# Linear attention and a PReLU layer in one kernel: the order of pieces in the usual steps

## The chip, the cores and the metric

The kernel runs on one core of a Trainium2 chip. The metric is device time in microseconds (us): the median of four runs before the change is 626.19 us (626.02 to 626.37). All views of the profile come from one further execution, recorded by the hardware profiler, which took 626.12 us. TensorE does the matmuls, VectorE (DVE) and ScalarE (ACT) do elementwise work, GpSimd (POOL) and SyncE (SP) mostly issue transfers (DMAs).

## The reference

Two blocks follow each other. The first is a linear attention with a forget gate: for 4 batches and 8 heads, over 768 tokens, with 48 x 48 states,

```
f = 1 / (1 + exp(-f_logit))
for t in range(S):
    state = f[:, :, t, :, None] * state + einsum('bhd,bhe->bhde', k[:, :, t], v[:, :, t])
    y[:, :, t] = einsum('bhd,bhde->bhe', q[:, :, t], state)
```

Its output, laid out as 3072 tokens of 384 numbers, is x of the second block:

```
h = x @ w_in                                     # 384 -> 2048
g = maximum(h, 0) + alpha * minimum(h, 0)
out = g @ w_out                                  # 2048 -> 384
```

All of it is in float32.

## The kernel before, in words

**Tiles and steps.** A step takes one chunk of 128 tokens for two batches and all heads, which makes 256 rows of x. There are 6 chunks and 2 pairs of batches, so 12 steps, numbered 0 to 11 here, the pairs alternating. In pass n of the main loop (called step n below) the attention of step n runs, the second block (the network) of step n-1, and the preparation of step n+1. A pass 12 has only the last network.

**Pieces.** Each part is a Python generator, and each `yield` ends a piece. The letters stand in the strings of orders.

- Q, preparation of the next step (`prepare`), 6 pieces. Piece 1 loads f, q, k and v by GpSimd's queue, applies the sigmoid, and makes the first products (ACT L267, L268, L270; DVE L278 to L282). Piece 2 has four ScalarE copies (L302) and two scans (L305, L307). Piece 3 has L309, L335 and the first L318; piece 4 has L362, L318 and L356; piece 5 has L386, the transpose L389, the last L318, L394, L356 and the four L402. Piece 6 has four ScalarE copies into the attention matrix A (L407) and sixteen DMAs on SP that write `ksn` from `kt` (L415). P is the same generator one step later, so a piece that Q left over is run as P.
- O, `carry`, 2 pieces: the `off` matmuls (L432) with four ScalarE copies into A (L450); then the `pd` matmuls (L472), which read `ksn` and give the state's update, whose first half DVE takes (L482, L486).
- S, `attend`, 6 pieces. Pieces 1 and 2, one for each batch of the pair: `raw` matmuls (L508), DVE's masked copies of them into `ad` (L514), `qu` matmuls (L523), and masked copies (L529). Pieces 3 and 4: four ScalarE copies each from `ad` to A (L551). Piece 5: the output matmuls `py` (L562). Piece 6, the output stage: the second half of the state's update (`moved(1)`, again L482 and L486), the ScalarE copies to y (L571), and the DMAs from y to xT on SP, ACT and POOL (L591).
- n, `network`, 13 pieces. Eight are hidden tiles: `ph` matmuls from xT (L606), ScalarE's negative part (L611, into one of two `neg` buffers), and two gate operations on DVE (L613), with four sums (L687) after the fourth and the eighth tile. Five make the output by seven products of 8 matmuls (L645), named pa, pb; pc, pd; pa, pc again; pe; with DVE and ScalarE combining them (L653, L658, L662, L663, L667 to L669, L672) and two stores by SP (L621).

**What sets the order.** On TensorE, DVE and ScalarE the order is exactly that in which the pieces issue their instructions: the schedule is manual for these three. SP and POOL are ordered by the framework. Steps 0 to 3 have orders of their own (`first`), steps 4 to 12 share `usual`. A piece that isn't there any more (the preparation in step 11, the attention in step 12) is passed over.

**Buffers that tie the pieces.** PSUM has two tiles of two banks (`pair`), used in turn by raw, qu, off, pd and py: `qu` at the head of a step takes the one that `pd` of the step before held, which is read last by L486. Four single banks serve ph and the products: the first `ph` of a step takes the bank of pc, last read by L667. `ksn` and y share one SBUF buffer, and f, q, k are loaded into single buffers.

Of the kernel before, what the change touches and what calls it, by code (L numbers as in the profile page):

```python
# [31 lines left out]
def kernel(  # L32
# [106 lines left out]
    for m in range(1, NB):  # L139
        lo = UO[m] + (4 if m == 1 else 0)  # L140
        n = NB - m
# [4 lines left out]
    for half in range(2):  # L146
        for m in range(1, NQ):
            n = NQ - m
# [540 lines left out]
    def halves_of_w_out():  # L689
# [23 lines left out]
        "P5 a w P a2 O w S w a w a2 S Q S O S w Q2 S Q2 S w",  # L713
        "a2 w b w O w n2 b2 v S P v2 n2 S b v Q n b n O S2 v n b v n Q2 b v Q b n S v2 W Q W S n2 W n W",
        "n S P n2 S n W n O Q n3 O S Q n S Q n Q S2 Q n3",
        "S n3 P S Q S n O n O n4 Q S Q S Q n S Q n3",
    )
    usual = "S n2 O P n S Q n2 Q n3 O n S2 n Q S Q2 S n3"
    pieces = {key: part for keys, parts in (("aw", load_weights(w_in_sb, w_in, "w_in")),
                                            ("bv", load_weights(w_out_sb, w_out, "w_out")))  # L720
              for key, part in zip(keys, parts)}
# [77 lines left out]
```

## Time and profile before

| What | Value |
|---|---|
| median of four runs | 626.19 us |
| the profiled execution | 626.12 us |
| its span on the core | 624.2 us |
| TensorE matmul busy | 589.3 us, 94% |
| VectorE busy | 502.4 us, 80% |
| ScalarE busy | 265.5 us, 43% |
| mean granted TensorE clock | 0.997 |
| HBM over the span | 66 GB/s |

The span runs from the first to the last instruction; the rest of the execution's time lies around it. A timeline row reads: start, time taken, engine, line, operation, output and inputs, shapes, how many; in brackets the idle time before it and what ended it. In rows of stages the columns are: the stretch, its length, busy time of TensorE matmuls, weight loads, VectorE, ScalarE and GpSimd, each with its count of instructions, then clock, share of DMA, and GB/s. One fp32 matmul of the program is two matmul records.

### The profile page before, as it was taken

To read this page: it belongs to the slowest core of one execution; us is meant where nothing else is said; L and a number is where in the kernel's file an instruction comes from. 1 tells how busy PE (TensorE), PEld (TensorE's weight loads), DVE (VectorE), ACT (ScalarE), POOL (GpSimd) and SP (SyncE) were. 2 spreads that over 40 slices of the span, in tenths; PEclk is the share of its full clock that TensorE was granted. 3 is DMA by queue.
4 is the path that set the end of the run, shared out by engine and by line. 5 is a ranking of instruction groups with operands and counts; after the bars stand their busy time and mean duration, and the time that the engine had idled before them with its cause. 6 is when DMAs were issued, how large, how long until landed. Compare 5 with 4: busy or idle time off the path is not lost.

```text
span 624.2 us, 19119 instructions
## 1 busy us (share of the span) xinstructions
PE 589.3 (94%) x8220; PEld 525.3 (84%) x8220; DVE 502.4 (80%) x1013; ACT 265.5 (43%) x482; POOL 60.5 (10%) x119
## 2 busy tenths in 40 slices
PE   3458999999999999999999999999999999999997
PEld 3346876789889899889889889889889889889997
DVE  7599889999799599699699699699799799673261
ACT  6797992371441541542442443353353353222110
POOL 8020001001001001001001001001001000000000
PEclk9998999999999999999999999999999999999999
DMA  8766614313314313413313323223222310300100
GB/s 308 269 226 193 194 43 96 76 35 88 85 36 94 78 35 86 85 36 85 64 59 85 56 68 85 54 68 83 54 73 73 64 38 13 65 4 13 41 0 26
DMA packets 68116, 50.43 MB, mean 81 GB/s; under 512 B 47168, under 2 KB 60608, under 8 KB 68032
## 3 DMA queue, kind: packets, MB, share of 16 engines
q1 hardware_dynamic: 56656, 25.01, 15.3%
q0 software_dynamic: 6864, 22.35, 12.3%
q10 hardware_dynamic: 4512, 1.85, 1.4%
q8 instruction: 65, 1.06, 0.7%
q14 instruction: 19, 0.16, 0.1%
HBM read 36.21 MB, written 4.72 MB: 66 GB/s over the span
## 4 chain that ended last, share of the span: by engine, by line
PE 68%; DVE 22%; ACT 7%; issue 1%; DMA 1%; ACTq 0%; DVEq 0%
PE ph L606 37%; PE pa L645 7%; PE pc L645 7%; PE pb L645 4%; DVE us L318 3%; PE qu L523 3%; PE pe L645 2%; PE pd L645 2%; PE raw L508 2%; DVE q L356 2%; DVE us L309 1%; DVE k L335 1%; DVE vs L486 1%; DVE kt L389 1%; PE pd L472 1%
## 5 line engine op out<-in xcount | busy, mean ns | idle before, releaser
L606 PE MATMUL ph<-xT,w_in_sb 128*128 128x256 f32 x1152 | 260.2, 385 | 0.0
L606 PEld LDWEIGHTS ph<-xT,w_in_sb 128*128 128x128 f32 x1152 | 217.6, 191 | 32.5 <-issue 2.5
L611 ACT ACTIVATE neg<-ph 128x512 f32<-128x512 f32 x96 | 57.2, 597 | 199.2 <-PE ph L606 152.1
L613 DVE SCALAR_TENSOR_TENSOR gate<-neg,om,ph 128x256 f32<-128x256 f32 x192 | 81.9, 475 | 58.6 <-ACT neg L611 58.6
L645 PE MATMUL pa<-w_out_sb,gate 128*128 128x192 f32 x352 | 63.5, 333 | 0.0
L645 PE MATMUL pc<-t,S 128*128 128x192 f32 x352 | 60.9, 327 | 0.0
L645 PEld LDWEIGHTS pa<-w_out_sb,gate 128*128 128x128 f32 x352 | 56.7, 190 | 2.2 <-DVE gate L613 0.7
L645 PEld LDWEIGHTS pc<-t,S 128*128 128x128 f32 x352 | 57.8, 191 | 0.1
L514 DVE COPY_PREDICATED ad<-mraw,raw 128x256 f32<-128x256 int32 (+1 forms) x96 | 42.4, 442 | 8.3 <-PE raw L508 5.8
L529 DVE COPY_PREDICATED ad<-mquad,qu 128x224 f32<-128x224 int32 (+6 forms) x140 | 41.9, 299 | 6.2
L551 ACT COPY A<-ad 32x256 f32<-32x256 f32 x96 | 38.6, 402 | 1.4
L571 ACT COPY y<-py 128x512 f32<-128x512 f32 x24 | 12.9, 588 | 58.0 <-PE py L562 57.9
L318 DVE TENSOR_TENSOR us<-us,fs 128x768 f32<-128x768 f32 (+5 forms) x60 | 36.8, 613 | 0.3
L302 ACT COPY us<-qd 128x256 f32<-128x256 f32 x48 | 29.8, 671 | 7.7 <-DVE qd L275 7.4
L687 DVE TENSOR_TENSOR S<-gate 128x512 f32<-128x512 f32 x44 | 30.3, 688 | 0.8
L645 PE MATMUL pb<-t,gate 128*128 128x192 f32 x176 | 30.4, 327 | 0.0
L645 PE MATMUL pd<-w_out_sb,S 128*128 128x192 f32 x176 | 30.4, 327 | 0.0
L645 PE MATMUL pe<-w_out_sb,S 128*128 128x192 f32 x176 | 30.4, 327 | 0.0
L508 PEld LDWEIGHTS raw<-qd,k 48*32 48x32 f32 x1536 | 18.3, 109 | 14.1 <-issue 8.5
L562 PEld LDWEIGHTS py<-A,vs 128*64 128x64 f32 x768 | 25.1, 145 | 5.8 <-issue 2.2
L407 ACT COPY A<-q 48x512 f32<-48x512 f32 x44 | 27.1, 617 | 6.4 <-DVE q L356 5.8
L508 PE MATMUL raw<-qd,k 48*32 48x80 f32 x1536 | 23.3, 244 | 6.9 <-ACT A L450 5.2
(109 smaller groups left out, 741.8 us busy)
## 6 DMA issues: line engine op xcount, KB each, us to landing
w_out_raw<-in_w_out SPq DMA_DIRECT2D x8, 767.8 KB, 4.6
w_in_raw<-in_w_in SPq DMA_DIRECT2D x8, 767.2 KB, 9.8
q<-in_qT POOLq DMA_DIRECT2D x11, 512.0 KB, 4.0
f<-in_fT POOLq DMA_DIRECT2D x11, 512.0 KB, 4.1
k<-in_kT POOLq DMA_DIRECT2D x11, 512.0 KB, 4.3
out<-o SPq DMA_DIRECT2D x24, 192.0 KB, 2.1
vs<-in_v POOLq DMA_DIRECT2D x22, 192.0 KB, 3.5
ksn<-kt SPq DMA_DIRECT2D x80, 32.0 KB, 2.0
```

What stands on the lines that cost most here:

```text
L302: nc.scalar.copy(q4[:, :, :, r], qdv[r][:, :, :, 0])
L318: nc.vector.tensor_tensor(us[:, :, UO[m]:UO[m] + 4 * n].rearrange("p g (i r) -> p g i r", r=4), us[:, :, skip:skip + 4 * n].rearrange("p g ...
L407: nc.scalar.copy(A[halves(cc)[1], :, par * HP:(par + 1) * HP, CH * cc:CH * (cc + 1)], q3[rows(par)].rearrange("p (u h c) s t -> p u h c (s ...
L508: nc.tensor.matmul(raw[DB * j:DB * (j + 1), par, hp * C:hp * C + QW], lhsT=k[r_, g * DB:(g + 1) * DB], rhs=qd[r_, g], start=True, stop=True)
L514: nc.vector.copy_predicated(adu[:, :, :, d:4], mraw[:, d, :, d:4].bitcast(I32).unsqueeze(1).broadcast_to((128, H, NB, n)), rv[:, :, QO[d]: ...
L529: nc.vector.copy_predicated(ad[:, u, :, :, 4 * m:DB], mquad[:, lo:lo + n].bitcast(I32).unsqueeze(1).unsqueeze(1).broadcast_to((128, 2, HP, ...
L551: nc.scalar.copy(A[s_, u, :, s_], ad[s_, u].rearrange("p r h t -> p (r h) t"))
L606: nc.tensor.matmul(ph[:, j * T:(j + 1) * T], lhsT=w_in_sb[:, kt, m * 128:(m + 1) * 128], rhs=xT[:, kt], start=(kt == 0 and j == 0), stop=( ...
L611: nc.scalar.activation(neg, phv, AF.Relu, scale=-1.0)
L613: nc.vector.scalar_tensor_tensor(gate[:, m % NH, m // NH], neg[:, j], om[:, m:m + 1], phv[:, j], ALU.mult, ALU.add)
L645: nc.tensor.matmul(to[:, 0:DH], lhsT=of(f), rhs=by(f), start=(f == 0 and not more), stop=(f == NH - 1), skip_group_check=True)
L687: nc.vector.tensor_tensor(to, x_, y_, op)
```

## The change

The strings of orders change; nothing else does. In the usual steps:

- The second attend piece comes before the `off` piece, and both carry pieces come between single hidden tiles, with no P.
- Preparation piece 1 comes after five hidden tiles (before: after three), piece 2 after all eight (before: after five), piece 3 right after the first output piece of the network and ahead of both copy pieces of attend.
- The copies to A and `py` (S3) come together ahead of pc and pd; before, `py` came after them.
- The output stage comes after preparation piece 4; before, it came after piece 5. Piece 5 and piece 6 follow within the same step, between the last pieces of the network.

Step 3 runs piece 6 ahead of its last two network pieces, so that step 4 finds it done.

```diff
         "n S P n2 S n W n O Q n3 O S Q n S Q n Q S2 Q n3",
-        "S n3 P S Q S n O n O n4 Q S Q S Q n S Q n3",
+        "S n3 P S Q S n O n O n4 Q S Q S Q n S Q n Q n2",
     )
-    usual = "S n2 O P n S Q n2 Q n3 O n S2 n Q S Q2 S n3"
+    usual = "S n2 S n O n O n Q n3 Q n Q S3 n Q S n Q n Q n"
```

## The prediction

> **What bounds the kernel now.** I read the engine shares and the chain on the page first, then cut the span into the kernel's steps (each from its first `raw` matmul to the next step's), then TensorE's rows at the seams, then the queues that feed them.
>
> ```profile
> PE 589.3 (94%) x8220; PEld 525.3 (84%) x8220; DVE 502.4 (80%) x1013; ACT 265.5 (43%) x482; POOL 60.5 (10%) x119
> ...
> PE 68%; DVE 22%; ACT 7%; issue 1%; DMA 1%; ACTq 0%; DVEq 0%
> ```
>
> TensorE bounds it; VectorE's 22% of the chain says that TensorE is held somewhere. By step (start:end, length, TensorE busy, its weight loads, VectorE):
>
> ```profile
> 155.27:202.65 47.38, 47.09 (x657) 42.73 (x657) 43.07 (x93) 17.89 (x35) 4.46 (x7) 1.00 0.31 71
> 202.65:249.56 46.91, 46.91 (x657) 42.62 (x656) 38.97 (x79) 18.48 (x35) 4.45 (x7) 1.00 0.26 66
> 249.56:297.28 47.72, 47.32 (x657) 42.64 (x657) 41.18 (x86) 18.54 (x35) 4.45 (x7) 1.00 0.29 68
> 297.28:344.97 47.69, 47.28 (x657) 42.64 (x656) 41.16 (x86) 18.54 (x35) 4.45 (x7) 1.00 0.27 68
> ...
> 487.71:535.05 47.34, 47.29 (x657) 42.64 (x656) 40.85 (x86) 18.57 (x35) 1.80 (x3) 1.00 0.18 39
> 535.05:581.87 46.82, 46.82 (x657) 42.82 (x657) 23.60 (x56) 13.43 (x28) 1.07 (x2) 1.00 0.14 30
> ```
>
> Step 3 is the first row; the usual order is used by steps 4 to 11, the others. Steps 4 to 10 take 332.40 us, 47.49 each. TensorE at a usual seam, then at the seam after step 3:
>
> ```profile
> 344.97 0.92 PE L508 MATMUL raw<-qd,k 48*32 48x80 f32 x64
> 346.29 1.08 PE L523 MATMUL qu<-us,k 48*32 48x112 f32 x64 [0.40 <-DVE vs L486]
> ```
> ```profile
> 186.93 1.27 PE L562 MATMUL py<-A,vs 128*64 128x64 f32 x36
> 188.49 1.04 PE L562 MATMUL py<-A,vs 128*64 128x64 f32 x28 [0.29 <-ACT A L551]
> ...
> 202.65 0.85 PE L508 MATMUL raw<-qd,k 48*32 48x80 f32 x60
> 203.28 0.26 PE L523 MATMUL qu<-us,k 48*32 48x112 f32 x1
> ```
>
> `qu` begins 1.32 after `raw` where 0.69 is its own pace (308.46 to 309.15): 0.63 lost, at five seams (steps 5 to 9); step 10 loses 0.28. The releaser is the state update of L486, which empties the `pd` bank that `qu` takes; in these steps it stands on VectorE behind preparation pieces 4 and 5. Step 3 runs it between them, and its seam has no wait; but its `py` waits on ScalarE's copies into A, since the copies of L302 stand ahead of them:
>
> ```profile
> 184.44 0.32 ACT L653 COPY Csum<-pa 128x192 f32<-128x192 f32 x1 [1.95 <-PE pa L645]
> 184.77 2.19 ACT L302 COPY us<-qd 128x256 f32<-128x256 f32 x4
> 186.76 1.68 ACT L551 COPY A<-ad 32x256 f32<-32x256 f32 x4
> ```
>
> **The change, part by part.** No instruction is added or removed; t counts from a step's first `raw`.
>
> *TensorE without waits.* Starts of one group to the next, from steps 3 and 6: raw 0.69, qu 1.00, ph0-1 5.38, raw 0.69, qu 1.00, ph2 2.79, off 0.68, ph3 2.79, pd 0.86, ph4-7 10.46 (three take 7.87, one more 2.59), pa 2.60, pb 2.69, py 2.01, pc 2.70, pd, pa and pc 2.60 each, pe 2.69: sum 46.83. The step is worth more only by what makes TensorE wait.
>
> *The seam (output stage sooner).* Old cost 0.63 x 5 + 0.28 = 3.43 us, plus up to 0.23 in `pa`, which waits in some steps for the last gates. New: L658 starts 0.27 after pc, then piece 4 (L362 to L318: 0.60+0.74+0.60+0.60+0.60+0.59 = 3.73), then L482/L486 (2.13); so L486 is done at t 43.1, and `qu` (t 47.9) doesn't wait for it. What is late next is `ph0`: its bank is emptied by L667, which now stands behind L662 and piece 5 (0.34+0.72+1.17+0.17+0.60+0.71+0.74 = 4.45). L667 ends at t 48.2, `ph0` of the next step starts at 48.9: 0.7 of slack. `qu` itself needs piece 5's last L318, done at 45.9.
>
> *Second attend half sooner.* raw at t 7.07 needs the four L514 of the first half, done at 3.8; off (11.55) needs the second four, done at 10.5; pd (15.0) needs the seven L529, done at 12.8. VectorE then idles until gate 3, so delays from before end here. Price nothing; a VectorE later by over 1.0 would show at off.
>
> *Piece 1 and the copies of L302, nearer to `py`.* This is where the new wait arises. ph3 starts at 12.23, and its ScalarE pass (L611) 2.95 later (547.34 to 550.29 in step 11): 15.18. From there VectorE is continuous: gate +0.63, its pair 0.91 to the sums, sums 2.64, L482/L486 2.19, gate pair 0.80, piece 1 3.60 (315.36 to 318.96), gate 5 ends 0.87 later. The L611 of ph7 needs that `neg` buffer, 0.11 later: 15.18 + 11.75 = 26.93. ScalarE then: L302 0.49 later (27.42), four L302 and L653 up to the first L551 2.26 (136.74 to 139.00), eight L551 3.34 (327.48 on): 33.02, TensorE awake 0.06 later at 33.08. `py` starts at 26.34 + 2.60 + 2.69 = 31.63 and comes to the matmul that needs the last L551 1.10 later, 32.73 (step 3 stopped at the same one). Wait 0.35, and 0.05 of restart as in step 3 (`py` 2.52 there, 2.01 elsewhere, for 0.46 of wait): 0.40. Bounds: nothing at all, and step 3's 0.51. I take 0.40, as its links are rows of the very instructions. Step: 46.83 + 0.40 = 47.23.
>
> *Piece 6 inside the step ahead.* ScalarE's four L407 (0.63 each) leave the place before ph2's L611, run at t 46.9 to 49.4 and finish before the next L611 (51.7): hidden under pe and the seam. SP: its program order becomes four of the sixteen `ksn` DMAs, store o1, twelve `ksn`, store o0 (before: seven, both stores, nine). So store o1's wait for L669 (t 48.8) now holds twelve `ksn` issues. Sixteen took 11.2 (4.84 + 6.38), 0.70 each: the last issues at 57.1, which is 9.9 of the next step, and lands 2.0 later (4.5 is the longest seen); pd wants it at 15.0. Hidden, by 3.1 or 0.6. The wait of the `ksn` writes for the xT DMAs (they read y, in the same buffer) is over by t 42.
>
> *DMAs that follow the moved pieces.* POOL's k load is issued after the second raw, at t 8.0 instead of 12.4 (309.68 in step 6); its readers come at 33. q goes out after L270 (t 22.1), f after L309 (33.4), vs and the xT moves after `py`: all 10 us or more ahead of their readers. xT leaves 3 us sooner than before, and ph0 did not wait for it then. Price nothing.
>
> ```profile
> k<-in_kT POOLq DMA_DIRECT2D x11, 512.0 KB, 4.3
> ...
> ksn<-kt SPq DMA_DIRECT2D x80, 32.0 KB, 2.0
> ```
>
> *Sum.* Step 4, which had no wait at its head: 47.23 - 46.91 = +0.32. Steps 5 to 9: 236.15 against 238.15, -2.00. Step 10: 47.23 against 47.34, -0.11. Step 11 has nothing to prepare, so no L302 and no wait, and its pe takes 2.60: 46.74 against 46.82, -0.08. Step 3 keeps its wait and its seam, step 12 is untouched. Total -1.87. The profiled execution took 626.12 (span 624.20 and 1.92 around it): 624.25. The median of the runs, 626.19, is 0.07 higher, within the spread of the runs: **624.3**.
>
> *Against a rule.* The seam's gap repeats, 0.40 to 0.41 idle at each. The Trainium skill (Perfetto Trace Analysis, Optimization Strategy) says that the same gap repeating on the engine that should be saturated can mean too little PSUM for the next tile. Taken so, an order that keeps two `pair` tiles keeps the gap, and the sum would be 0.40 x 7 - 0.1, or 2.7 more than now, some 628.8, against 624.3 by the rows. Step 3 has the same two tiles and no gap, so I follow the row.
>
> **The rivals.**
>
> *The copies come in time.* If the ScalarE run is 0.4 shorter, TensorE never waits: 46.83 a step, 7 x 46.83 + 46.74 = 374.6 against 332.40 + 46.82 = 379.2: 621.5. For it: the wait is the difference of two sums of some 33 us. Against: step 3 waited.
>
> *The wait is as in step 3 or longer.* 0.51 gives 47.34 a step, a gain of 1.1, 625.0; with 0.66 the step is the old mean, and all is given back: 626.1. For it: eight copies stand behind L302, where step 3 had four. Against: there L302 began only after L653, here before it.
>
> *Nothing is removed.* If VectorE reaches L486 too late after all, the seam stays: 626 to 629. Against: 4.8 us of slack.
>
> *Slower: `ksn` lands late.* The k load now runs at t 8.0 to 13, across the last `ksn` DMAs, which no usual step of before shows. If the last `ksn` is held for the whole 4.3 of the k load, it lands at 9.9 + 2.0 + 4.3 = 16.2, pd waits 1.2, and the `py` wait shrinks to the 0.05: step 48.08, +4.1 in all, 630.2. It decides from a pd wait of about 0.8, a landing 6 us after its issue; the longest seen is 4.5. The Trainium skill (DMA: Bandwidth & Descriptors, Issuing engines are not separate DMA queues) says that DMAs of all issuers interleave on the same sixteen engines; with that page's fit (Anatomy of one DMA) of 2.0 us plus bytes over 436 GB/s the k load would, as an estimate, hold the others for 1.2, not 4.3, and pd would not wait: 624.3 again. No row of this trace shows the two together.
>
> **How the numbers follow.** Forecast (a `py` wait of 0.25 to 0.5) 0.52; copies in time 0.13; a longer wait 0.17; nothing removed 0.05; `ksn` late or another late wait 0.13. A measurement of this kernel tells about 0.2%, 1.25 us, from no change, so faster ends at 624.9, a wait of 0.49. Faster: 0.46 of the forecast and 0.13, 0.59; same: 0.06 + 0.17 + 0.05, 0.28; slower 0.13. Range 621.5 (no wait) to 626.2 (all given back), leaving out the late `ksn`; the forecast's own is 623.2 to 625.0.
>
> **What would show it.** Right: `qu` starts 0.69 to 0.7 after `raw` in steps 5 to 10, without L486 as releaser; a wait of 0.2 to 0.3 idle in `py` on A (L551) in steps 4 to 10, none in step 11; steps of 47.1 to 47.35 us; the four L302 just ahead of L653. Wrong: `py` waiting 0.5 or more, a wait of `ph` on L667 or of `pd` on `ksn`, or steps of 46.9.

## The result, and the profile after

| | median | lowest to highest | runs |
|---|---|---|---|
| kernel before | 626.30 us | 624.27 to 628.31 | 71 |
| changed kernel | 625.13 us | 623.38 to 626.76 | 46 |

The ratio is 0.9981, with a 95% interval of 0.9976 to 0.9987: 0.8 to 1.5 us are gone, at about the 0.2% that this kernel can be told by. The forecast was 624.3, in a range of 621.5 to 626.2. The profiled execution has a span of 623.2 us, 1.0 below that of before.

The page of the changed kernel, shares of the engines and of the chain that ended last:

```profile
PE 588.0 (94%) x8220; PEld 525.7 (84%) x8220; DVE 503.1 (81%) x1013; ACT 260.5 (42%) x482; POOL 62.7 (10%) x119
PE 61%; DVE 19%; ACT 14%; issue 4%; DMA 1%; ACTq 0%; DVEq 0%
```

VectorE's share of the chain fell from 22 to 19%, ScalarE's rose from 7 to 14%: one wait has gone and another has come. The stages of the changed kernel, steps 3, 4, 6, 7, 10 and 11 (start:end, length, TensorE busy, weight loads, VectorE, ScalarE, GpSimd, clock, DMA share, GB/s):

```profile
155.30:202.68 47.38, 47.10 (x657) 42.73 (x656) 42.95 (x92) 20.26 (x39) 4.46 (x7) 1.00 0.31 71
202.68:249.90 47.22, 47.07 (x657) 42.71 (x657) 40.04 (x79) 15.55 (x33) 4.46 (x7) 1.00 0.28 66
...
297.24:344.61 47.37, 47.25 (x657) 42.88 (x656) 41.25 (x86) 17.80 (x36) 4.45 (x7) 1.00 0.29 68
344.61:392.01 47.40, 47.26 (x657) 42.87 (x657) 41.29 (x86) 17.79 (x36) 4.46 (x7) 1.00 0.31 69
...
486.52:533.85 47.33, 47.20 (x657) 42.83 (x656) 39.93 (x85) 19.97 (x39) 1.80 (x3) 1.00 0.19 40
533.85:580.84 46.99, 46.99 (x657) 42.87 (x657) 23.64 (x55) 11.11 (x25) 1.07 (x2) 1.00 0.13 29
```

Step 3 is as it was. Steps 4 to 11 take 378.16 us (580.84 less 202.68) against 379.22 before: 1.06 less, where 1.87 was forecast. A usual step is 47.22 to 47.40 where before had one of 46.91, five near 47.6 and one of 47.3.

TensorE's timeline of the changed kernel at the seam into step 6:

```profile
297.24 0.85 PE L508 MATMUL raw<-qd,k 48*32 48x80 f32 x60
...
297.96 1.16 PE L523 MATMUL qu<-us,k 48*32 48x112 f32 x62
299.05 0.48 PE L606 MATMUL ph<-xT,w_in_sb 128*128 128x256 f32 x1
```

`qu` begins inside the run of `raw`, 0.64 to 0.72 after it, and no bracket names L486: the seam wait is gone. VectorE ahead of this seam:

```profile
291.98 1.12 DVE L486 TENSOR_TENSOR vs<-vs,pd 48x384 f32<-48x384 f32 x2
...
297.83 0.36 DVE L667 TENSOR_TENSOR Csum<-pc,Csum 128x192 f32<-128x192 f32 x1
```

L486 ends at 293.10, 4.8 ahead of `qu`. The price is to be seen on ScalarE, and then on TensorE, in the same step:

```profile
324.33 0.60 ACT L611 ACTIVATE neg<-ph 128x512 f32<-128x512 f32 x1 [2.35 <-DVE gate L613]
324.82 2.18 ACT L302 COPY us<-qd 128x256 f32<-128x256 f32 x4
326.79 0.37 ACT L653 COPY Csum<-pa 128x192 f32<-128x192 f32 x1
327.07 3.33 ACT L551 COPY A<-ad 32x256 f32<-32x256 f32 x8
```
```profile
329.06 2.43 PE L562 MATMUL py<-A,vs 128*64 128x64 f32 x64
331.42 0.76 PE L645 MATMUL pc<-t,S 128*128 128x192 f32 x3
```

L302, L653 and the eight copies run without a gap, the last copy ends at 330.40, and `py` lasts 2.36 (329.06 to 331.42) instead of 2.01. The releaser that the waits of the weight loads name (in all, times, longest; from step 4 on) is the copy; a wait of up to 0.3 in seven of eight steps:

```profile
PEld py L562 <- ACT A L551: 1.8, 7, 0.3
```

### The profile page after: what moved, and what is told of

Its sections match the earlier page's. It is cut to its first block, busy times and chain, and to the rows that moved or that the text cites. A ratio compares the mean times of both kernels' runs of the same rounds, so it can differ in the third digit from the quotient of the medians.

```text
span 623.2 us, 19118 instructions
## 1 busy us (share of the span) xinstructions
PE 588.0 (94%) x8220; PEld 525.7 (84%) x8220; DVE 503.1 (81%) x1013; ACT 260.5 (42%) x482; POOL 62.7 (10%) x119
## 3 DMA queue, kind: packets, MB, share of 16 engines
q0 software_dynamic: 6864, 22.35, 12.5%
q8 instruction: 65, 1.06, 0.7%
## 4 chain that ended last, share of the span: by engine, by line
PE 61%; DVE 19%; ACT 14%; issue 4%; DMA 1%; ACTq 0%; DVEq 0%
PE ph L606 25%; PE pc L645 9%; PE pa L645 6%; PE pe L645 5%; PE pd L645 5%; ACT A L551 4%; ACT us L302 3%; DVE gate L613 3%; PE qu L523 3%; DVE S L687 3%; PE raw L508 3%; DVE qd L275 3%; PE py L562 2%; ACT neg L611 2%; DVE vs L482 1%
## 5 line engine op out<-in xcount | busy, mean ns | idle before, releaser
L645 PE MATMUL pa<-w_out_sb,gate 128*128 128x192 f32 x352 | 61.0, 327 | 0.0
L645 PEld LDWEIGHTS pa<-w_out_sb,gate 128*128 128x128 f32 x352 | 58.0, 190 | 0.6
L663 ACT COPY o<-pa 128x192 f32<-128x192 f32 x11 | 3.5, 318 | 75.3 <-PE pa L645 72.3
L562 PE MATMUL py<-A,vs 128*64 128x64 f32 x768 | 28.8, 233 | 3.4 <-ACT vs L488 1.3
L508 PEld LDWEIGHTS raw<-qd,k 48*32 48x32 f32 x1536 | 18.4, 109 | 13.9 <-issue 8.3
```

What stands on the lines that cost most here:

```text
L508: nc.tensor.matmul(raw[DB * j:DB * (j + 1), par, hp * C:hp * C + QW], lhsT=k[r_, g * DB:(g + 1) * DB], rhs=qd[r_, g], start=True, stop=True)
L562: nc.tensor.matmul(py[64 * par:64 * par + 64, u, o:o + CH], lhsT=vs[bp][:, cc, u, hd * D:hd * D + 64], rhs=A[:, u, par * HP + hp, CH * cc: ...
L645: nc.tensor.matmul(to[:, 0:DH], lhsT=of(f), rhs=by(f), start=(f == 0 and not more), stop=(f == NH - 1), skip_group_check=True)
```

## The experiments

All are orders of the same pieces. "The changed line" is

```
usual = "S n2 S n O n O n Q n3 Q n Q S3 n Q S n Q n Q n"
```

and `first[3]` is step 3's line. The sums below are read from the traces like those above; "head" is the time from a step's first `raw` to its first `ph` (1.69 without a wait).

| Kernel | steps 4 to 11, us | ratio to before (95%) |
|---|---|---|
| before | 379.22 | |
| changed | 378.16 | 0.9981 (0.9976 to 0.9987) |
| changed, once more | 378.22 | 0.9993 (0.9981 to 1.0004) |
| output stage alone | 377.22 | 0.9958 (0.9943 to 0.9973) |
| piece 6 in the next step | 378.63 | 0.9980 (0.9970 to 0.9990) |
| copies behind L653, L302 | 390.59 | 1.0173 (1.0144 to 1.0202) |
| L653 behind the copies | 376.46 | 0.9951 (0.9936 to 0.9967) |
| copies first | 376.13 | 0.9933 (0.9920 to 0.9947) |
| copies first, step 3 too | 375.56 | 0.9937 (0.9921 to 0.9953) |
| the same, once more | 375.87 | 0.9939 (0.9926 to 0.9952) |
| the same, k load later | 376.30 | 0.9944 (0.9927 to 0.9960) |
| the same, `off` beside `pd` | 380.75 | 1.0015 (1.0004 to 1.0026) |

**The output stage alone** (against the kernel before). Theory: the seam gap is the order on VectorE. Rival: too few `pair` tiles.

```diff
-    usual = "S n2 O P n S Q n2 Q n3 O n S2 n Q S Q2 S n3"
+    usual = "S n2 O P n S Q n2 Q n3 O n S2 n Q S Q S Q n3"
```

> The order of before with one move: the last gated output piece of a usual step (L658, L662, L667) stands ahead of preparation piece 4 instead of behind piece 5; pieces 1, 3 and 6 stay where before had them, and so does L302 on ScalarE. My theory (the seam gap was only the order on VectorE): L486 ends some 4 us ahead of qu, so qu begins 0.69 to 0.71 after raw in steps 5 to 10 without L486 as its releaser, and 0.63 a step comes back there. What is late next is L667, since VectorE has a longer run behind it: a wait of ph0 on L667 of 0 to 0.4. Steps 5 to 9 at 47.0 to 47.4 instead of 47.6, no py wait on A; 624.0 to 625.3 in all, ratio 0.9965 to 0.999. Rival (too few pair tiles in PSUM, whatever the order): the gap of 0.4 before qu stays or moves to ph0 in full, and the time stays at 626.3 within 0.5.

Measured: 624.31 us, ratio 0.9958. No wait on L486 is left, with the same two tiles; the rival falls. What is late next is L667, as the theory had it. VectorE of this kernel at the seam into step 6, and its weight loads' waits from step 4 on:

```profile
297.91 0.72 DVE L402 TENSOR_TENSOR f<-ps 48x8 f32<-48x8 f32 x4
298.64 0.36 DVE L662 TENSOR_TENSOR o<-Csum,pd 128x192 f32<-128x192 f32 x1
298.91 0.35 DVE L667 TENSOR_TENSOR Csum<-pc,Csum 128x192 f32<-128x192 f32 x1
```
```profile
PEld ph L606 <- DVE Csum L667: 2.2, 6, 0.4
...
PEld pa L645 <- DVE gate L613: 0.9, 4, 0.2
```

L667 ends at 299.26 and `ph` starts at 299.32, which makes the head 1.94, 0.25 over its own pace, in five steps. (The edit moves the output stage behind preparation piece 4; the lines that the expectation names for it, L658, L662 and L667, belong to the network.) The surprise is that this one move beats the whole change. Its waits are smaller: 1.36 at the heads and 1.15 in `pa`, 2.51 in all; in the changed kernel 0.52 at the heads, 0.32 in the second `raw` and `qu`, 2.64 in `py`, 3.48. Without them the steps of both take 46.84: (377.22 - 2.51) / 8 and (378.16 - 3.48) / 8. The wait in `pa` is counted from 2.70, since this is what it takes right behind the small matmuls of `pd` when no gate is late (behind `ph` it takes 2.60). Step 11 of this kernel, from 559.70 to 562.40:

```profile
558.84 0.94 PE L472 MATMUL pd<-vs,ksn 64*48 64x48 f32 x64
559.70 2.87 PE L645 MATMUL pa<-w_out_sb,gate 128*128 128x192 f32 x16
562.40 2.76 PE L645 MATMUL pb<-t,gate 128*128 128x192 f32 x16
```

In the other usual steps it takes 2.78 to 2.93.

**Piece 6 back in the next step.**

```diff
-        "S n3 P S Q S n O n O n4 Q S Q S Q n S Q n Q n2",
+        "S n3 P S Q S n O n O n4 Q S Q S Q n S Q n3",
-    usual = "S n2 S n O n O n Q n3 Q n Q S3 n Q S n Q n Q n"
+    usual = "S n2 P S n O n O n Q n3 Q n Q S3 n Q S n Q n2"
```

> The changed kernel with preparation piece 6 (four L407 on ScalarE, its ksn DMAs on SP) back at the head of the next step, as before had it; the output stage and pieces 1 to 5 stay as the change put them. My theory (completing the preparation inside the step ahead neither costs nor gains, all of it is covered): within 0.4 us of the changed kernel, 624.7 to 625.5, ratio to before 0.9975 to 0.9988; qu at 0.69 to 0.71, py at 2.3 to 2.4 as there. It also shows whether qu0's 1.07 to 1.10 instead of 1.00 in steps 5 to 10 comes from piece 6's work beside it: at 1.00 the steps would be 0.1 shorter and the time 0.6 lower. Rival (the ksn DMAs between the stores cost something): 1 us or more below the changed kernel; rival (completing the preparation early is where the gain comes from): back at 626.3.

Measured: 625.55 us, ratio 0.9980, that of the changed kernel. Completing the preparation inside the step ahead neither gains nor costs in the time. The heads are 1.71 to 1.81, so the small excess of `qu` there doesn't come from piece 6. One step has a `pd` of 1.48 instead of 0.87 with `ksn` as its releaser; its `py` takes 2.07, nearly without a wait, as the prediction's rival said it would.

**The copies later.** Theory: `py` waits for the end of the ScalarE run, so what is put ahead adds one for one.

```diff
-    usual = "S n2 S n O n O n Q n3 Q n Q S3 n Q S n Q n Q n"
+    usual = "S n2 S n O n O n Q n3 n Q2 S3 n Q S n Q n Q n"
```

> The changed kernel with the pass of ph7 (L611), which waits for its neg buffer, issued ahead of L302 and the eight A copies in such an order that L302 stands behind L653, as in step 3. My theory (py waits for the end of the ScalarE run L302, L653, L551, so what is put ahead of it adds one for one): the first L551 begins some 2 us later than in the changed kernel, the last ends at 35, py waits some 2.2 instead of 0.3 in steps 4 to 10: 12 to 14 us more than the changed kernel, 637 to 639, ratio to before 1.017 to 1.021. Rival (py's loss is not that run): 625 within 0.5. Between the two, if L302 starts as soon as in the changed kernel because its operands come no later: a wait of 0.3 to 1, 625 to 630.

Measured: 637.36 us, ratio 1.0173. ScalarE, then TensorE, of step 6 of this kernel:

```profile
330.04 0.32 ACT L653 COPY Csum<-pa 128x192 f32<-128x192 f32 x1 [1.64 <-PE pa L645]
330.25 2.20 ACT L302 COPY us<-qd 128x256 f32<-128x256 f32 x4
332.24 3.36 ACT L551 COPY A<-ad 32x256 f32<-32x256 f32 x8
```
```profile
333.13 0.34 PE L562 MATMUL py<-A,vs 128*64 128x64 f32 x4 [0.53 <-ACT A L551]
333.97 1.18 PE L562 MATMUL py<-A,vs 128*64 128x64 f32 x32 [0.50 <-ACT A L551]
335.65 1.03 PE L562 MATMUL py<-A,vs 128*64 128x64 f32 x28 [0.50 <-ACT A L551]
```

The last copy ends at 335.60, 34.9 after the step's start at 300.66 (35 was expected). `py` starts 0.59 late (3.29 after `pb` instead of 2.69) and takes 3.49 instead of 2.01: 2.07 a step. Steps 4 to 11 are 12.43 longer than in the changed kernel, of 12 to 14 expected.

**L653 behind the copies.** The copies stand behind two things, L302 and L653. Which of them?

```diff
-    usual = "S n2 S n O n O n Q n3 Q n Q S3 n Q S n Q n Q n"
+    usual = "S n2 S n O n O n Q n3 Q S2 n Q S n Q S n Q n Q n"
```

> The changed kernel with the eight copies into A (L551) issued between the copies of L302 and L653: L302 stays ahead of them, L653 (which waits for pa and takes 0.3) goes behind. It asks which of the two makes py late. Theory A, from the rows of the changed kernel (L302 ends at t 29.6 and L653, let go by pa at 29.2, would end at 29.6 without it, so each alone holds the copies to about 29.6 and both to 29.8): py takes 2.15 to 2.25 in steps 4 to 10 instead of 2.32 to 2.38, as step 11, which has L653 but no L302, takes 2.21; 0.8 to 1.2 us below the changed kernel, ratio to before 0.9960 to 0.9972. Theory B (L302 alone, as I predicted): py stays at 2.3 to 2.4 and the time at that of the changed kernel. Theory C (L653 alone): py 2.01 and 2.3 us or more.

Measured: 623.94 us, ratio 0.9951. ScalarE and `py` in step 6 of this kernel:

```profile
325.40 2.19 ACT L302 COPY us<-qd 128x256 f32<-128x256 f32 x4
327.35 3.36 ACT L551 COPY A<-ad 32x256 f32<-32x256 f32 x8
330.74 0.32 ACT L653 COPY Csum<-pa 128x192 f32<-128x192 f32 x1
```
```profile
329.61 2.19 PE L562 MATMUL py<-A,vs 128*64 128x64 f32 x64
331.73 1.57 PE L645 MATMUL pc<-t,S 128*128 128x192 f32 x8
```

`py` takes 2.12 to 2.15 in six of the seven usual steps (here 329.61 to 331.73), so L302 alone makes 0.11 to 0.14 of the 0.31 to 0.37. In step 7 it takes 2.01, behind a `pd` of 1.17. And in step 11, which has no L302, `py` falls from 2.21 to 2.02 with L653 out of the way: L653 alone makes 0.2. Theory A is the nearest, neither B nor C, though `py` lies a little under its 2.15 to 2.25; steps 4 to 11 are 1.70 shorter than in the changed kernel, more than its 0.8 to 1.2.

**The copies first.** Both out of the way: the last four copies ahead of the pass of ph6.

```diff
-    usual = "S n2 S n O n O n Q n3 Q n Q S3 n Q S n Q n Q n"
+    usual = "S n2 S n O n O n Q n S2 n2 Q n Q S n Q S n Q n Q n"
```

> The changed kernel with one move: the last four copies into A (L551) are issued ahead of the pass of ph6 (L611) and of L302 and L653 instead of behind them. My theory (py waits because L302 and L653 run ahead of the last A copies on ScalarE): the last L551 ends 2 us or more before py comes to it, py takes 2.01 again in steps 4 to 10 instead of 2.32 to 2.38, no releaser L551 is left in the usual steps, and 0.3 to 0.35 a step come back: 2.1 to 2.5 us less than the changed kernel, 622.6 to 623.0, ratio to before 0.994 to 0.9955. Rival (the longer py is not that queue but slower matmuls, or another operand): py stays above 2.25 and the time at 625.1 within 0.4; second rival: the copies' price moves to another wait (L653 later holds pa, L611 of ph6 later holds a neg buffer), and the gain is under 0.8.

Measured: 622.94 us, ratio 0.9933. ScalarE in step 7 of this kernel:

```profile
366.36 0.59 ACT L611 ACTIVATE neg<-ph 128x512 f32<-128x512 f32 x1
366.85 3.32 ACT L551 COPY A<-ad 32x256 f32<-32x256 f32 x8
...
371.85 2.19 ACT L302 COPY us<-qd 128x256 f32<-128x256 f32 x4
373.83 0.37 ACT L653 COPY Csum<-pa 128x192 f32<-128x192 f32 x1
```

The copies end at 370.17, 5.8 ahead of `py` (375.96), which takes 2.01 or 2.02 in all usual steps. Nothing else became late but the head of step 11, by 0.1, and `pd` in step 5, and the latter is the wait that the prediction named as the slower rival. TensorE of this kernel there:

```profile
264.66 0.30 PE L472 MATMUL pd<-vs,ksn 64*48 64x48 f32 x6
265.35 0.89 PE L472 MATMUL pd<-vs,ksn 64*48 64x48 f32 x58 [0.39 <-DMA ksn<-kt]
```

It costs 0.63 (1.50 for 0.87); with no `py` wait behind it, the step pays it in full: 47.57 between neighbours of 46.86 and 46.99.

**Step 3 too.** In the next kernels step 3's copies are also put ahead of its L653 and L302.

```diff
-        "S n3 P S Q S n O n O n4 Q S Q S Q n S Q n Q n2",
+        "S n3 P S Q S n O n S O n4 Q2 S Q n S Q n Q n2",
-    usual = "S n2 S n O n O n Q n3 Q n Q S3 n Q S n Q n Q n"
+    usual = "S n2 S n O n O n Q n S2 n2 Q n Q S n Q S n Q n Q n"
```

> The kernel with the copies ahead of ph6, and the same done in step 3, whose copies into A now also stand ahead of L653 and of the copies of L302. My theory (the same queue on ScalarE makes py of step 3 wait): py of step 3 takes 2.01 instead of 2.49 to 2.52, step 3 lasts 46.8 to 46.9 instead of 47.3 to 47.4, and no wait of py on L551 is left in the main loop: 0.5 us below the kernel with the copies ahead of ph6, ratio to before 0.992 to 0.9935. Rival: step 3's wait has another cause (its preparation is in another state, since step 2 still halves the output weights), and py stays at 2.5.

Measured: 622.31 us, ratio 0.9937, and once more, beside other runs of the kernel before, 622.50 and 0.9939. Steps 3 and 4 of the first:

```profile
154.59:201.44 46.85, 46.85 (x657) 42.57 (x656) 43.13 (x94) 19.97 (x39) 4.47 (x7) 1.00 0.32 71
201.44:248.29 46.85, 46.85 (x658) 42.57 (x657) 40.19 (x80) 16.19 (x33) 4.47 (x7) 1.00 0.28 68
```

Step 3 lost its 0.5, so its `py` wait had the same cause. The times can't tell the 0.5 from the kernel above; the intervals lie over each other. TensorE is busy throughout these two steps, at the prediction's 46.83. In the first run no step has a long `pd`, in the second step 5 has one of 1.09.

> The kernel with the copies ahead of ph6 in steps 3 and up once more, beside the one with off moved: ratio to before 0.992 to 0.995, as in its first run; steps of 46.84 to 47.04, but for one with a pd wait on ksn of up to 0.6 if the late ksn comes and goes.

**The k load later.** Is it the k load that makes `ksn` late?

```diff
-    usual = "S n2 S n O n O n Q n S2 n2 Q n Q S n Q S n Q n Q n"
+    usual = "S n2 O n S n O n Q n S2 n2 Q n Q S n Q S n Q n Q n"
```

> The kernel with the copies ahead of ph6 in all steps from 3 on, and the second half of attend (raw, qu) back behind off and ph2, where before had it, so that the k load is issued at t 10.5 or later instead of 8. It asks whether the k load is what made a pd wait 0.6 for ksn in one step of two of the runs. My theory (the k load runs across the last ksn DMAs): longest ksn landing in each step 3.0 or less until the k load starts, no pd wait on ksn, the usual steps 46.85 to 47.0 without an exception; 0.3 to 0.7 below the kernel with the k load at 8 where that shows the pd wait, the same within 0.3 where not; ratio to before 0.991 to 0.993. Rival (SP's own issues are what comes late: 12 in a row, some of 1 to 2.4 us, whatever the k load does): the last ksn is issued at t 11 to 12.5 as there and a pd wait of 0.4 to 0.6 stays in some step.

Measured: 623.06 us, ratio 0.9944. GpSimd's queue in step 6, of the changed kernel and of this one:

```profile
305.69 0.73 POOL L254 DMA_DIRECT2D k<-in_kT  x1 [18.49 <-PE raw L508]
```
```profile
309.48 0.73 POOL L254 DMA_DIRECT2D k<-in_kT  x1 [21.42 <-PE raw L508]
```

That is t 8.45 and 11.87. The longest landing of a `ksn` DMA in each of steps 5 to 10 is 3.6 to 3.9 with the late k load, where 3.0 or less was expected; with the early one it is 3.8 to 5.5 in five steps of the changed kernel, and 4.2 to 5.2 in six of its best variant. The last `ksn` is issued at t 10.5 to 10.9, against 9.6 to 11.6 and 10.5 to 12.2 in those two, so SP's issues were held a little less as well. No step has a long `pd`. How a k load holds a `ksn` can be read from the landings. In step 7 of the changed kernel the k load is issued at t 8.46 and lands at 13.93; the `ksn` issued at 8.64 lands at 14.12, 5.5 after its issue, where 2.0 is the median. In the twelve traces, all 37 `ksn` DMAs of steps 4 to 10 that were issued up to 0.7 behind a k load, and whose landing is recorded, landed 0.2 to 0.4 behind that load. So they are held until it is over, as the prediction's slower rival had it. The estimate of 1.2 by the Trainium skill (DMA: Bandwidth & Descriptors, Anatomy of one DMA) does not agree with these rows. But the hold counts from the k load's issue at t 8.4, not from that of the last `ksn`, and in the changed kernel it is over by t 12.5 to 13.9, ahead of `pd` at 15. The `ksn` that made `pd` wait landed later still: in step 7 of the changed kernel's second run at t 15.46, the k load at 12.86. What held that one is open, so this run does not show that the k load makes `pd` wait. The gain was not there either: `raw` is later, VectorE gets to the gates later, and `pa` takes 2.63 to 2.94 instead of 2.60. One wait was traded for another, and the time is the same.

**The changed kernel once more,** beside the three kernels above:

> The changed kernel as it is, beside the three others of this call: 0.9976 to 0.9987 of before again, and 3 us above the kernel with the copies ahead.

Measured: 626.23 us, ratio 0.9993. That is above the 0.9976 to 0.9987 expected, and the interval reaches 1.0004, so from these twelve runs alone nothing could be said of a gain. In the profile, steps 4 to 11 take 378.22, as before; what is longer stands ahead of them (step 4 begins at 204.29 instead of 202.68). The difference to the best kernel beside it is 3.9 us of medians (626.23 less 622.31), where 3 was expected. Also, step 7 has a `pd` of 1.25 and a `py` of 2.08, step length 47.40: here a late `ksn` costs nearly nothing, since `py` would have waited anyway.

**`off` beside `pd`.** If every return from small matmuls to `ph` costs 0.1, one return less should gain. This is set against the kernel with step 3 too. The expectation's 46.72 for the order with only the output stage sooner takes `pa` at 2.60 there; with the 2.70 shown above, both orders come to some 46.83, and there was no 0.1 to explain. The price of a return can be tested all the same.

```diff
-    usual = "S n2 S n O n O n Q n S2 n2 Q n Q S n Q S n Q n Q n"
+    usual = "S n2 S n2 O2 n Q n S2 n2 Q n Q S n Q S n Q n Q n"
```

> The kernel with the copies ahead of ph6 in steps 3 and up, and with the matmuls of off set behind ph3, next to pd, so that TensorE leaves the network's matmuls for the small ones once less in each usual step. It asks why the order with only the output stage sooner beat the changed kernel although it kept waits of its own: there pd stood next to pa, and TensorE's groups without waits summed to 46.72 where the changed order's sum to 46.83 (ph0-1 5.38, off 0.69, ph2 2.79, raw 0.69, qu 1.00, ph3-7 13.15, pd 0.86, which is 24.56, against 24.67). My theory (each return from small matmuls to ph costs 0.1): ph2-3 take 5.38 in place of 2.79 twice, the usual steps 46.73 to 46.95 instead of 46.84 to 47.04, 0.6 to 1.0 below the kernel it is set against, ratio to before 0.991 to 0.9925. Rival: the groups keep their sum, the time is the same within 0.3; rival on the other side: A copies of off (L450) now stand ahead of later ScalarE passes, and py or pa waits again, 0.1 or more a step.

Measured: 627.25 us, ratio 1.0015: 4.75 us the wrong way. TensorE in step 7 of this kernel, then of the changed kernel:

```profile
359.63 0.76 PE L432 MATMUL off<-q,kh 48*32 48x32 f32 x64
360.47 1.58 PE L472 MATMUL pd<-vs,ksn 64*48 64x48 f32 x64
361.98 2.21 PE L606 MATMUL ph<-xT,w_in_sb 128*128 128x256 f32 x9
```
```profile
359.81 0.94 PE L472 MATMUL pd<-vs,ksn 64*48 64x48 f32 x64
360.68 0.70 PE L606 MATMUL ph<-xT,w_in_sb 128*128 128x256 f32 x2
```

ph2 and ph3 in one run take 5.38 instead of 2.79 twice, so a return does cost 0.2. But `pd` takes 1.51 to 1.66 right behind `off`, and 0.87 behind `ph`, in all eight steps, and `off` 0.82 to 0.85 instead of 0.69. No releaser stands at it. In step 7 the trace shows a stop of 0.28 ahead of `pd`'s first matmul and stops of 0.18 at its second, third and fourth, where the matmuls of `pd` otherwise start 0.05 apart at most. In the program, just these four carry the waits for the sixteen `ksn` DMAs, about four waits each, and the last of these DMAs had landed 0.36 ahead of `pd`. That TensorE's sequencer works through those waits under the long `ph` matmuls, and has no such cover behind `off`, would fit; it is argued and was not tested.

## Why the prediction was right, and where its size was off

- *TensorE without waits, 46.83.* Right: with the waits gone steps take 46.84 to 47.04, but for those with a late `ksn`.
- *The seam, 3.43 us.* Right in cause: L486 no longer holds `qu`, in any step; ahead of step 6 it was done at t 43.2 (43.1 forecast). It gave back a little less: the heads are 1.69 in steps 4 and 8 and 1.72 to 1.82 in the others, 0.52 over their pace in all. In four of the steps the trace shows two stops of about 0.06 within `qu`, and no releaser. They are in all kernels with this order, with piece 6 in either place; their cause stays open. The second `raw` and `qu` were 0.32 longer in all.
- *L667's slack of 0.7.* Right: it ended at 298.19 in step 6's seam, t 48.3 of the step before (48.2 forecast), and the start of `ph` shows the same 0.19 after the last `qu` in every step. The move of the output stage without the others lost this slack, and 0.25 a step with it.
- *The new `py` wait, 0.40.* Nearly right in size: 0.31 to 0.37, 2.44 in seven steps where 2.80 was summed. The walk of numbers was off by 0.2 at most: L302 at t 27.58 (27.42), last copy's end at 33.16 (33.02), start of `py` at 31.82 (31.63). Half right in cause: the prediction blamed L302; L653, which waits for `pa`, holds the copies to almost the same moment.
- *Step 11, "no L302 and no wait".* Wrong: L653 alone left 0.20. The step took 46.99 for 46.74.
- *`ksn` hidden by 3.1 or 0.6.* Too wide. In steps 5 to 10 the last of the sixteen is issued at t 9.6 to 11.6, not 9.9, and one landed 5.5 after its issue, beyond the 4.5 taken as the longest. Nor was it so that no row of before shows a k load and a `ksn` together: both landings of 4.5 there are such rows. In step 9 the k load was issued at t 12.45, the `ksn` 0.5 later, and it landed 0.2 behind the load; there `pd` came at t 26.1, so nothing waited. The slower rival is real, in one step of some executions, at 0.2 to 0.6; in the changed kernel the `py` wait covers it, as the rival said.
- *The sum.* -1.87 was forecast for steps 4 to 11, -1.06 came, a little over half. The terms: heads +0.52, second halves +0.32, `py` -0.36, step 11's `py` +0.20, which is 0.68 of the 0.81; the other 0.13 is in differences of 0.01 to 0.02 a step in the rows. That the `py` wait came out smaller hid part of the other three, which is luck.
- *The rule against it.* The Trainium skill (Perfetto Trace Analysis, Optimization Strategy) has a repeating gap as a possible sign of too few buffers, which made 628.8. The gap vanished with the same two tiles, by order alone; in this case the row of step 3, not the rule, told it.

What the prediction did not ask is what each move was worth by itself. The one that only moves the output stage takes 0.94 less in steps 4 to 11 than the change as a whole, as its waits that are left come to 2.51 against 3.48, and 2.64 of the latter is the `py` wait that the other moves bring. The change with its copies taken ahead in the queue is faster still. The full change with the copies first takes 0.9933 to 0.9939 of the time before, the fastest that was run.

## What to carry to other kernels

When one engine's queue is reordered to end a wait, walk the queue of every engine that feeds the next wait: an in-order engine passes on the lateness of whatever stands in front, and two things in front (here L302 and an L653 that waits for TensorE) can each be enough, so taking out one gains only a part. Test such a cause by dose: put the suspect behind, ahead, and twice as far, and see whether the wait follows. Count a wait from what the group takes in the same surroundings without one, or the price of a neighbour is taken for a wait. A move that is "off the path" still sets when transfers start and which matmuls follow which; with `off` beside `pd` this cost 4.88 in steps 4 to 11, more than the 3.43 of the wait that was removed.

## What the runs showed that was not expected

- The same transfers took longer after the reorder. Before, the xT DMAs landed after 3.4 (SP) and 3.8 us (ACT), and v after 3.5, in the median; in the changed kernel after 4.6, 5.1 and 4.7. In steps 4 to 11 nobody waited for them.
- A small DMA issued on SP just behind a load of 512 KB on GpSimd's queue landed only 0.2 to 0.4 us behind that load, up to 6.0 us after its issue instead of 2.0.
- The same 64 `pd` matmuls took 0.87 us behind `ph` and 1.51 to 1.66 behind `off`, without a named wait.
- A group of small matmuls set between two `ph` tiles costs beside its own time: two tiles take 5.38 in one run and 2.79 each when parted.
